# Where an attention pair's high part is made, and when one operand's copy is taken, in a fused attention and two-MoE kernel

## The chip, the cores and the metric

The kernel runs on one core of a Trainium2 chip. The metric is the device time of one execution in microseconds, lower is better. The engines are TensorE (PE in the rows, PEld for its weight loads), VectorE (DVE), ScalarE (ACT), GpSimd (POOL) and SyncE (SP), whose queue issues nearly all transfers.

## What is computed

Attention with a decay, then a mixture of experts with one expert for each token, then a dense two-layer network. Only the attention is touched. Cut from the reference:

```python
def _attn_ref(q, k, v, f):                      # q, k, v: 4 x 8 x 576 x 64
    scores = scale * np.matmul(q, k.transpose(0, 1, 3, 2))
    cum = np.cumsum(np.log(np.clip(f, 0.0001, 1.0)), axis=-1)
    scores = np.where(causal, -1e9, scores + cum[..., :, None] - cum[..., None, :])
    attn = np.exp(scores - np.max(scores, axis=-1, keepdims=True))
    attn = attn / (np.sum(attn, axis=-1, keepdims=True) + 1e-09)
    return np.matmul(attn, v)
x = attn_out.transpose(0, 2, 1, 3).reshape(B * S, H * D)
x = _moe_ref(x, ...)                            # 8 experts, the best one for each token
return _moe2_ref(x, ...)                        # (max(0.01 h, h)) @ w_out, h = x @ w_in
```

## The kernel before

**Pairs of heads.** The 32 heads (4 batches of 8) are worked through as 16 pairs, g = 0 to 15. The 576 rows of a head are five row blocks: 0 to 3 of 128 rows, block 4 of 64 (both heads' block 4 share one tile). A pair's scores come in four groups: blocks 0 and 1 together (`qk01`), then 4, 2 and 3. For each group TensorE forms scores in PSUM (L331, L332, with the mask L334 or L337), VectorE takes the row maxima (`nm`, L341, and L388 for block 4), ScalarE takes exponentials with their row sums (L346, L393). Then TensorE transposes the probabilities (L420, L410), ScalarE copies the transposes to SBUF (L422, L412), and TensorE multiplies them with the values (L432).

**High and low parts.** Scores are made from q and k in two parts. `prep_hi(g)` makes the high part `aq` of a loaded pair on VectorE (L299). It also issues, on SP, three small transfers (L301, L302) and the transfer of half of `aq` to `bk` (L303), and on POOL two copies into the tile for block 4 (L305). `prep_lo(g)` then takes `ak`'s copy of half of `aq` on ScalarE (L312) and the low part on VectorE (L313). On SP it issues L314, L315 and L316, the last of which overwrites the half of `aq` that L312 and L303 read; on POOL one copy (L317).

**Output stage.** `xout(g)` runs a pair later. It sums and inverts the row sums (L448 to L450), TensorE turns the products back (L455), in two halves (row blocks 0 to 2, then 3 and 4), and VectorE scales each half out of PSUM with two instructions, into `x` and into `lp` for the gate (L459).

**Buffers.** The transposes and both halves of the output stage take PSUM tiles in turn from a pool of three (`pst`). So the second transposes of row block 3 use the buffer that the first half of the output stage has to leave. Score tiles take turns in a pool of two (`psc`): the scores of row block 2 use the buffer of blocks 0 and 1, once the exponentials of these have read it.

**Order.** In the attention loop PE, ACT, DVE and SP run in the order in which the code is written; POOL's order is left to the scheduler. For each pair the loop calls `first`, `last`, `third`, `fourth`. `first(g)` makes the scores of blocks 0 and 1 and transposes row block 3 of the pair before (two tiles, four transposes each). `fourth(g)` makes block 3's scores, the transposes of block 2, and the output stage of the pair before; `prep_hi` of the pair two ahead stands in it too. The other halves of the kernel, the experts and the dense network, follow the loop and keep their order.

Of the kernel before, what the change touches and what calls it, by code (L numbers as in the profile page):

```python
# [73 lines left out]
def fused(ctx: ExitStack, tc, qk0, qk2, vp, f, mid, wg, mb, w1, w2, w_in, w_out, out):  # L74
# [71 lines left out]
    with tc.tile_pool(name="pst", bufs=PST, space=PSUM) as pst:  # L146
# [44 lines left out]
        def vload(g):  # L191
            vts[g] = a2.tile([P, 2, NC, D], F32, tag="vt", name=f"vt{g}", bufs=2)
            nc.sync.dma_start(vts[g], vp[:, 2 * g:2 * g + 2])

        def load(g):
            if g == 1:

                xt[0] = pe.tile([P, NC, XW], F32, tag="x", name="x0")
                raw = xt[0].rearrange("p c d -> p (c d)")[:, :2 * S].rearrange("p (h s) -> p h s", h=2)
            else:  # L200
                raw = pe.tile([P, 2, S], F32, tag="raw", name=f"raw{g}", bufs=3)
            nc.sync.dma_start(raw, qk2[:, 2 * g:2 * g + 2, :])
            ops[g] = raw
# [90 lines left out]
        def prep_hi(g):  # L294
            raw = ops[g]
            aq, ak = (aqk.tile([P, 2, S], F32R, tag=n, name=f"{n}{g}") for n in ("aq", "ak"))
            h = aq.bitcast(F32)
            bq, bk, a4, b4 = bqs[g % NBUF], bks[g % NBUF], aq4[g % NBUF], bq4[g % NBUF]
            nc.vector.tensor_scalar(aq, raw, qs, None, ALU.mult)  # L299
            for t, r0, c0 in ((bq, 64, 0), (bk, 66, 2)):  # L300
                nc.sync.dma_start(t[r0:r0 + 2].bitcast(F32), agd[c0:c0 + 2, 2 * g:2 * g + 2, :])  # L301
            nc.sync.dma_start(b4[64:66, :, :64].bitcast(F32), agd[0:2, 2 * g:2 * g + 2, 4 * P:])  # L302
            nc.sync.dma_start(bk[0:64].bitcast(F32), h[64:128])  # L303
            for r in (0, 64):
                nc.gpsimd.tensor_copy(a4[r:r + 64, :, :64], h[0:64, :, 4 * P:])  # L305
            ops[g] = (raw, aq, ak)

        def prep_lo(g):
            raw, aq, ak = ops[g]
            bq, bk, b4 = bqs[g % NBUF], bks[g % NBUF], bq4[g % NBUF]  # L310
            h = aq.bitcast(F32)
            nc.scalar.copy(ak[0:64], h[64:128])  # L312
            nc.vector.scalar_tensor_tensor(raw.bitcast(F32R), raw, qs, h, ALU.mult, ALU.subtract)  # L313
            nc.sync.dma_start(bq[0:64].bitcast(F32), raw[0:64])  # L314
            nc.sync.dma_start(ak[64:128].bitcast(F32), raw[64:128])  # L315
            preps.append(nc.sync.dma_start(h[64:128], h[0:64]))  # L316
            nc.gpsimd.tensor_copy(b4[0:64, :, :64], raw[0:64, :, 4 * P:])  # L317
            ops[g] = (aq, bq, ak, bk)
# [30 lines left out]
        def qk01(g):  # L349
            sc = psc.tile([P, 2, 512], F32, tag="sc", name=f"sc{g}_01")  # L350
            vs = [sc[:, c, :2 * (c + 1) * P].rearrange("p (j k) -> p j k", j=2) for c in range(2)]
            for c, v in enumerate(vs):
                scores(g, c, v)
            nms = [maxima(g, c, v) for c, v in enumerate(vs)]

            def then():
                pt = a3.tile([P, 2, 3 * P], F32, tag="p0", name=f"p{g}_01", bufs=2)
                for c, v in enumerate(vs):
                    exps(g, c, v, nms[c], pt[:, :, c * P:(2 * c + 1) * P])
                    yield  # L360
            return then()

        def qk(g, c):
            n = (c + 1) * P
            view = psc.tile([P, 2, 512], F32, tag="sc", name=f"sc{g}_{c}")[:, :, :n]
            scores(g, c, view)
            nm = maxima(g, c, view)

            def then():
                exps(g, c, view, nm, a3.tile([P, 2, 4 * P], F32, tag="p", name=f"p{g}_{c}", bufs=2)[:, :, :n])  # L370
            return then
# [25 lines left out]
        def part_of(g, part):  # L397
            if (g, part) not in st:
                st[g, part] = a2.tile([P, 2, (3, NC)[part], (XA, XB)[part]], F32, tag=f"t{part}", name=f"tt{g}_{part}", bufs=2 - part)
            return st[g, part]  # L400


        def tr(g, c, js):
            sb = part_of(g, c // 3)
            if c == 4:
                pt = st.pop((g, c, "p"))
                for b0, b1 in ((0, 3), (3, 5)):
                    ps = pst.tile([P, 512], F32, tag="t", name=f"pt{g}_4_{b0}")
                    for b in range(b0, b1):
                        nc.tensor.transpose(ps[:, (b - b0) * P:(b - b0 + 1) * P], pt[:, b * P:(b + 1) * P], ident)  # L410
                    i = ps[:, :(b1 - b0) * P].rearrange("p (b j q) -> p j b q", j=2, q=64)
                    nc.scalar.copy(sb[:, :, b0:b1, P:], i)  # L412
                return
            pt = st[g, c, "p"]
            ps = pst.tile([P, 512], F32, tag="t", name=f"pt{g}_{c}_{js[0]}")
            nb = c + 1
            for i, j in enumerate(js):
                for b in range(nb):
                    k = i * nb + b
                    nc.tensor.transpose(ps[:, k * P:(k + 1) * P], pt[:, j, b * P:(b + 1) * P], ident)  # L420
            o = sb[:, js[0]:js[-1] + 1, 0:nb, c % 3 * P:(c % 3 + 1) * P]
            return lambda: nc.scalar.copy(o, ps[:, :len(js) * nb * P].rearrange("p (j b q) -> p j b q", b=nb, q=P))  # L422
# [14 lines left out]
            st[g, "x", part] = xu  # L437
            nc.vector.tensor_copy(xu[:, :w], pv_[:, :w])

        def xout(g):  # L440
            b, gg = divmod(g, H // 2)
            if gg == 0 and b:
                xt[b] = (pe, pre)[b % 2].tile([P, NC, XW], F32, tag="x", name=f"x{b}")
            x = xt[b]
            lp = lps[b % 2]
            rr = a3.tile([P, NC, 2], F32, tag="rr", name=f"rr{g}")

            nc.vector.tensor_copy(sms[g % 3][:64, 4, 1:2], sms[g % 3][64:, 4, 0:1])  # L448
            nc.vector.tensor_scalar(rr, sms[g % 3], 1e-9, None, ALU.add)
            nc.vector.reciprocal(rr, rr)  # L450
            for part, c0, n in ((0, 0, 3), (1, 3, 2)):
                xu = st.pop((g, "x", part))
                ps = pst.tile([P, 512], F32, tag="t", name=f"xo{g}_{part}")
                for i in range(n):
                    nc.tensor.matmul(ps[:, i * HW:(i + 1) * HW], lhsT=xu[:, i * P:(i + 1) * P], rhs=idw[:, gg, :], start=True, stop=True)  # L455
                i0 = ps[:, :n * HW].rearrange("p (c d) -> p c d", d=HW)
                sc = rr[:, c0:c0 + n, :].unsqueeze(3)
                for o, a, w in ((x[:, c0:c0 + n, gg * P:(gg + 1) * P], slice(0, P), D), (lp[:, c0:c0 + n, gg, :], slice(P, HW), E)):
                    nc.vector.tensor_tensor(o.rearrange("p c (j d) -> p c j d", j=2), i0[:, :, a].rearrange("p c (j d) -> p c j d", j=2), sc.to_broadcast([P, n, 2, w]), ALU.mult)  # L459
            if gg == H // 2 - 1:  # L460
                routing.append(route(b))
                if b == B - 2:
                    routing.append(route1(pre, (B - 1) * NC))
# [80 lines left out]
        def store(n):  # L544
            for _ in range(min(n, len(stores))):
                b, x, c0, c1 = stores.pop(0)
                t0 = b * S + c0 * P
                if c0 == 4:
                    nc.sync.dma_start(xs[t0:(b + 1) * S, :], x[:64, 4, :])
                else:  # L550
                    nc.sync.dma_start(xs[t0:t0 + (c1 - c0) * P, :].rearrange("(c p) d -> p c d", p=P), x[:, c0:c1, :])
# [91 lines left out]
        NG = BH // 2  # L643
# [10 lines left out]
        def first(g):  # L654
            then = qk01(g) if g < NG else None
            cs = [tr(g - 1, 3, (j, )) for j in range(2)] if g else ()
            if g + 1 < NG:
                prep_lo(g + 1)
            store(1 + (g > 12))
            for c in cs:  # L660
                c()
            for _ in then or ():
                pass

# [21 lines left out]
        def fourth(g):  # L686
            then = qk(g, 3) if g < NG else None
            if g + 3 < NG:
                load(g + 3)
            if g + 1 < NG:  # L690
                vload(g + 1)
            if g + 2 < NG:
                prep_hi(g + 2)
            cs = [tr(g, 2, (j, )) for j in range(2)] if then else ()
            for c in cs:
                c()
            if g:
                xout(g - 1)
            if then:
                then()  # L700

# [530 lines left out]
```

## Time and profile before

| | us |
|---|---|
| median of 3 runs | 890.97 |
| lowest, highest | 889.01, 891.54 |
| profiled execution | 889.86 |
| its span, first to last instruction | 888.2 |
| TensorE busy in the span | 853.8 (96%) |
| attention loop from the second pair on | about 24 to 208 of the span |

The rows further down are from one profiled execution. A row of the timeline is: start in us from the span's start, duration in us, engine, line of the kernel, operation, out<-in with the tile names (buffer numbers left out), shape, count of merged instructions, and in brackets the idle time just before on that engine with what ended it. A busy TensorE is not TensorE at its peak, since its instructions overlap.

### The profile page before, as it was taken

Reading aid. Unit: us, or ns where it says so; the run is one execution under the profiler, and the core shown is the slowest. Engines: PE = TensorE matmul, PEld = TensorE weight load, DVE = VectorE, ACT = ScalarE, POOL = GpSimd, SP = SyncE. Lnnn points to the kernel's source line nnn. Section 1 sums busy time; section 2 is a strip of 40 time slices with the busy share of each in tenths; the row PEclk is TensorE's granted clock in tenths of the full one; section 3 lists DMA queues with packets and bytes.
Section 4 is the critical chain, followed back from the end, with each engine's and each line's share of the span. In section 5 each row is a group of like instructions: output and inputs, shape, how many; then the busy total and the mean of one; then the engine's idle time right before and its main releaser. Section 6 shows DMA issues by size and latency. Waiting matters only on the chain. (4 is left out here: it accounts for less than half of the span.)

```text
span 888.2 us, 14348 instructions
## 1 busy us (share of the span) xinstructions
PE 853.8 (96%) x4733; PEld 704.4 (79%) x4733; DVE 601.7 (68%) x1070; ACT 503.7 (57%) x969; POOL 124.9 (14%) x185
## 2 busy tenths in 40 slices
PE   5999999998999999999999999999999999999996
PEld 4788787886788788888787788888888888888885
DVE  6678777886748999999985373386337943473333
ACT  5787778776348899999975353453223422242221
POOL 5000000001112314532231000000000000001112
PEclk9999999999999999999999999999999999999998
DMA  5776786766278145121322240032001300011111
GB/s 153 222 175 183 204 201 180 203 174 221 74 229 285 53 155 166 55 71 51 107 96 64 59 143 13 1 106 84 1 1 48 119 24 0 1 48 48 48 47 72
DMA packets 32994, 92.91 MB, mean 105 GB/s; under 512 B 7349, under 2 KB 8021, under 8 KB 32914
## 3 DMA queue, kind: packets, MB, share of 16 engines
q1 hardware_dynamic: 28082, 76.70, 29.8%
q0 software_dynamic: 4800, 15.23, 5.4%
q8 instruction: 39, 0.64, 0.3%
q14 instruction: 41, 0.34, 0.1%
q10 hardware_dynamic: 32, 0.01, 0.0%
HBM read 132.09 MB, written 14.99 MB: 166 GB/s over the span
## 5 line engine op out<-in xcount | busy, mean ns | idle before, releaser
L1124 ACT COPY us<-u 128x512 f32<-128x512 f32 (+1 forms) x80 | 43.6, 544 | 162.6 <-PE u L1122 162.5
L1125 DVE SCALAR_TENSOR_TENSOR us<-u,us 128x512 f32<-128x512 f32 (+1 forms) x80 | 51.0, 638 | 124.7 <-ACT us L1124 123.1
L1122 PE MATMUL u<-fxl,whii 128*128 128x512 f32 (+1 forms) x320 | 118.0, 369 | 0.0
L1122 PE MATMUL u<-fxh,wloi 128*128 128x512 f32 (+1 forms) x320 | 117.9, 368 | 0.0
L1122 PE MATMUL u<-fxh,whii 128*128 128x512 f32 (+1 forms) x320 | 116.8, 369 | 0.7 <-ACT fxh L764 0.7
L1142 PE MATMUL a<-whio,gh 128*128 128x512 f32 x280 | 109.6, 392 | 0.0
L1142 PE MATMUL a<-wloo,gh 128*128 128x512 f32 x280 | 109.2, 390 | 0.0
L1142 PE MATMUL a<-whio,gl 128*128 128x512 f32 x280 | 103.2, 389 | 0.0
L876 DVE TENSOR_TENSOR w1l<-w1r,w1h 128x1024 fp32r<-128x1024 f32 x72 | 86.3, 1221 | 10.8 <-ACT w1h L875 8.3
L346 ACT ACTIVATE p<-sc,nm 128x128 f32<-128x128 f32 (+3 forms) x128 | 66.2, 527 | 28.9 <-DVE nm L341 27.2
L876 DVE TENSOR_TENSOR w2l<-w2r,w2h 128x1024 fp32r<-128x1024 f32 x68 | 80.2, 1218 | 0.8 <-ACT w2h L875 0.7
L1127 ACT CAST gh<-us 128x512 fp32r<-128x512 f32 (+1 forms) x76 | 44.6, 587 | 58.1 <-DVE us L1125 38.5
L875 ACT CAST w1h<-w1r 128x1024 fp32r<-128x1024 f32 x72 | 73.7, 1055 | 3.6 <-PE h L893 3.6
L1128 DVE TENSOR_TENSOR gl<-us,gh 128x512 fp32r<-128x512 f32 (+1 forms) x76 | 49.3, 648 | 38.5 <-ACT gh L1127 36.4
L875 ACT CAST w2h<-w2r 128x1024 fp32r<-128x1024 f32 x68 | 69.5, 1052 | 4.4 <-PE y L921 2.3
L1122 PEld LDWEIGHTS u<-fxh,whii 128*128 128x128 f32 x320 | 60.2, 188 | 11.0 <-ACT fxh L764 0.9
L1122 PEld LDWEIGHTS u<-fxh,wloi 128*128 128x128 f32 x320 | 60.3, 188 | 10.3
L1122 PEld LDWEIGHTS u<-fxl,whii 128*128 128x128 f32 x320 | 60.3, 188 | 10.3
L341 DVE TENSOR_REDUCE nm<-sc 128x2 f32<-128x256 f32 (+1 forms) x64 | 51.1, 820 | 23.4 <-PE sc L337 21.3
L921 PE MATMUL y<-w2h,hh 128*128 128x512 f32 x160 | 64.8, 405 | 0.0
L1152 POOL DMA_INDIRECT out<-acc,tid x18 | 18.0, 997 | 326.0 <-DVE acc L1149 287.5
L921 PE MATMUL y<-w2h,hl 128*128 128x512 f32 x160 | 63.1, 395 | 0.2 <-DVE hl L914 0.2
(275 smaller groups left out, 1807.6 us busy)
## 6 DMA issues: line engine op xcount, KB each, us to landing
w1r<-w SPq DMA_DIRECT2D x88, 512.0 KB
w2r<-w SPq DMA_DIRECT2D x82, 512.0 KB
rwi<-w_in SPq DMA_DIRECT2D x16, 512.0 KB
rwo<-w_out SPq DMA_DIRECT2D x16, 512.0 KB
raw<-qk SPq DMA_DIRECT2D x14, 576.0 KB
vt<-vp SPq DMA_DIRECT2D x16, 320.0 KB
xr<-yd SPq DMA_DIRECT2D x18, 256.5 KB
bk<-aq SPq DMA_DIRECT2D x15, 288.0 KB
```

What stands on the lines that cost most here:

```text
L341: nc.vector.tensor_reduce(nm, view, axis=AX.X, op=ALU.max, negate=True)
L346: st["exp"] = nc.scalar.activation(pt[:, j, :], view[:, j, :], AF.Exp, bias=nm[:, j:j + 1], scale=1.0, accum_out=sms[g % 3][:, c, j:j + 1])
L875: nc.scalar.copy(hi[k], raw[k])
L876: nc.vector.tensor_tensor(lo[k], raw[k], hi[k].bitcast(F32), ALU.subtract)
L921: nc.tensor.matmul(Yp[t], lhsT=ap[:, k * P:(k + 1) * P], rhs=wp[k // 2][:, k % 2, :], start=(k == 0 and i == 0), stop=(k == NFB - 1 and i ...
L1122: nc.tensor.matmul(ps, lhsT=w[:, c], rhs=x[:, k, :], start=(k == 0 and i == 0), stop=(k == NKB - 1 and i == 2))
L1124: nc.scalar.copy(us, ps)
L1125: nc.vector.scalar_tensor_tensor(us, ps, 0.01, us, ALU.mult, ALU.max)
L1127: nc.scalar.copy(gh, us)
L1128: nc.vector.tensor_sub(gl, us, gh.bitcast(F32))
L1142: nc.tensor.matmul(A[b][i], lhsT=x[:, c], rhs=w, start=(first and m == 0), stop=(last and m == 2))
L1152: d = nc.gpsimd.indirect_dma_start(out=out[:, :], out_offset=bass.IndirectOffsetOnAxis(ap=tid[:, c:c + 1], axis=0), in_=Y[b, i], in_offset ...
```

## The change

Two orders are changed; no instruction is added or removed. `xout` takes a function to call between its halves, and `fourth(g)` hands it `prep_hi(g + 2)`. So the high part, which stood ahead of the transposes of block 2 in the code and thereby ahead of the whole output stage on VectorE, now stands behind the first half's scaling. In `fourth(0)`, which has no output stage, it is called in place. In `first(g)` the copies of the transposes of row block 3 now stand ahead of `prep_lo(g + 1)`, and so ahead of L312.

```diff
-        def xout(g):
+        def xout(g, between=None):
...
+                if part == 0 and between:
+                    between()
...
             cs = [tr(g - 1, 3, (j, )) for j in range(2)] if g else ()
+            for c in cs:
+                c()
             if g + 1 < NG:
                 prep_lo(g + 1)
             store(1 + (g > 12))
-            for c in cs:
-                c()
...
-            if g + 2 < NG:
-                prep_hi(g + 2)
             cs = [tr(g, 2, (j, )) for j in range(2)] if then else ()
             for c in cs:
                 c()
+            hi = (lambda: prep_hi(g + 2)) if g + 2 < NG else None
             if g:
-                xout(g - 1)
+                xout(g - 1, hi)
+            elif hi:
+                hi()
```

The order on TensorE, POOL and SP is the same as before in the whole program. On VectorE 13 instructions move (g = 1 to 13) and on ScalarE 14 (g = 1 to 14).

VectorE in `fourth(1)`, from the maxima of row block 3 to the first maxima of the next pair. `sm` are the row sums, `rr` their inverses, `xo_0` and `xo_1` the two halves in PSUM. Before:

```order
L341 TENSOR_REDUCE nm_3_490<-sc_3_483 128x2
L299 TENSOR_SCALAR aq_496<-raw_350,qs 128x1152
L448 COPY sm_184<-sm_184 64x1
L449 TENSOR_SCALAR rr_515<-sm_184 128x10
L450 RECIPROCAL rr_515<-rr_515 128x10
L459 TENSOR_TENSOR x_209<-xo_0_519,rr_515 128x3x128
L459 TENSOR_TENSOR lp_191<-xo_0_519,rr_515 128x3x16
L459 TENSOR_TENSOR x_209<-xo_1_525,rr_515 128x2x128
L459 TENSOR_TENSOR lp_191<-xo_1_525,rr_515 128x2x16
```

The same place on VectorE after the change:

```order
L341 TENSOR_REDUCE nm_3_490<-sc_3_483 128x2
L448 COPY sm_184<-sm_184 64x1
L449 TENSOR_SCALAR rr_506<-sm_184 128x10
L450 RECIPROCAL rr_506<-rr_506 128x10
L459 TENSOR_TENSOR x_209<-xo_0_510,rr_506 128x3x128
L459 TENSOR_TENSOR lp_191<-xo_0_510,rr_506 128x3x16
L299 TENSOR_SCALAR aq_516<-raw_350,qs 128x1152
L459 TENSOR_TENSOR x_209<-xo_1_525,rr_506 128x2x128
L459 TENSOR_TENSOR lp_191<-xo_1_525,rr_506 128x2x16
```

L299 moved behind the two instructions that empty `xo_0`.

ScalarE around `first(2)`, from the exponentials of row block 3 of pair 1 (`p_3`) to those of blocks 0 and 1 of pair 2 (`p_01`); `pt_3_0` and `pt_3_1` are the two tiles of transposes, `tt_1` where they go. Before:

```order
L346 ACTIVATE p_3_530,sm_185<-sc_3_483,nm_3_490 128x512 x2
L312 CAST ak_497<-aq_496 64x1152
L422 COPY tt_1_548<-pt_3_0_549 128x4x128
L422 COPY tt_1_548<-pt_3_1_554 128x4x128
L346 ACTIVATE p_01_567,sm_186<-sc_01_533,nm_0_544 128x128 x2
```

The same place on ScalarE after the change:

```order
L346 ACTIVATE p_3_530,sm_185<-sc_3_483,nm_3_490 128x512 x2
L422 COPY tt_1_548<-pt_3_0_549 128x4x128
L422 COPY tt_1_548<-pt_3_1_554 128x4x128
L312 CAST ak_517<-aq_516 64x1152
L346 ACTIVATE p_01_567,sm_186<-sc_01_533,nm_0_544 128x128 x2
```

L312 moved behind the two copies, directly ahead of the exponentials.

## Rows read from the trace of the kernel before

**Rows 1.** Waits, 24 to 204 us: engine, line <- releaser: total us, times, longest.

```profile
PE pt L420 <- DVE lp L459: 2.0, 8, 0.4
```

**Rows 2.** Timeline of TensorE, pair 8, transposes of block 3 to the products.

```profile
109.89 0.60 PE L420 MATMUL pt<-ident,p 128*128 128x128 f32 x4
110.70 0.63 PE L420 MATMUL pt<-ident,p 128*128 128x128 f32 x4 [0.22 <-DVE lp L459]
...
114.40 0.44 PE L331 MATMUL sc<-ak,aq 128*128 128x384 f32 x1
...
115.43 1.64 PE L432 MATMUL pv<-tt,vt 128*64 128x192 f32 x20
```

**Rows 3.** Timeline of VectorE, same place: high part, and the first half's last instruction.

```profile
108.27 0.81 DVE L299 TENSOR_SCALAR aq<-raw,qs 128x1152 fp32r<-128x1152 f32 x1
...
110.36 0.20 DVE L459 TENSOR_TENSOR lp<-xo,rr 128x48 f32<-128x48 f32 x1
```

**Rows 4.** Timeline of ScalarE, pair 8, cast to the copies of block 4.

```profile
109.63 0.20 ACT L346 ACTIVATION_READ_ACCUMULATOR p<-sc,nm 128x1 f32 x1
109.86 1.15 ACT L312 CAST ak<-aq 64x1152 fp32r<-64x1152 f32 x1
110.92 1.06 ACT L422 COPY tt<-pt 128x512 f32<-128x512 f32 x2
111.98 0.37 ACT L346 ACTIVATE p<-sc,nm 128x128 f32<-128x128 f32 x1
...
113.49 0.21 ACT L346 ACTIVATION_READ_ACCUMULATOR p<-sc,nm 128x1 f32 x1
113.58 0.76 ACT L412 COPY tt<-pt 128x384 f32<-128x384 f32 x2
```

**Rows 5.** Timeline of TensorE, pair 14: first transposes of block 3, scores of block 2.

```profile
183.91 0.60 PE L420 MATMUL pt<-ident,p 128*128 128x128 f32 x4
...
188.00 0.44 PE L331 MATMUL sc<-ak,aq 128*128 128x384 f32 x1
```

**Rows 6.** Timeline of ScalarE, pair 14: first copy of those transposes.

```profile
184.60 0.59 ACT L422 COPY tt<-pt 128x512 f32<-128x512 f32 x1 [0.35 <-PE pt L420]
```

**Rows 7.** Timeline of ScalarE, pair 7: second copy and first exponential.

```profile
99.56 0.59 ACT L422 COPY tt<-pt 128x512 f32<-128x512 f32 x1
100.17 0.37 ACT L346 ACTIVATE p<-sc,nm 128x128 f32<-128x128 f32 x1
```

**Rows 8.** Timeline of TensorE, pair 9: first transposes of block 3, scores of block 2.

```profile
121.80 0.60 PE L420 MATMUL pt<-ident,p 128*128 128x128 f32 x4
...
126.68 0.44 PE L331 MATMUL sc<-ak,aq 128*128 128x384 f32 x1 [0.30 <-ACT p L346]
```

**Rows 9.** Timeline of ScalarE, pair 9: first and last of the exponentials' rows.

```profile
124.90 0.37 ACT L346 ACTIVATE p<-sc,nm 128x128 f32<-128x128 f32 x1 [1.02 <-DVE nm L341]
...
126.41 0.21 ACT L346 ACTIVATION_READ_ACCUMULATOR p<-sc,nm 128x1 f32 x1
```

**Rows 10.** Timeline of TensorE, pairs 1, 2 and 4, the same two places.

```profile
24.68 1.04 PE L420 MATMUL pt<-ident,p 128*128 128x128 f32 x8
...
29.63 0.44 PE L331 MATMUL sc<-ak,aq 128*128 128x384 f32 x1 [0.33 <-ACT p L346]
...
37.01 0.60 PE L420 MATMUL pt<-ident,p 128*128 128x128 f32 x4
38.03 0.63 PE L420 MATMUL pt<-ident,p 128*128 128x128 f32 x4 [0.42 <-DVE lp L459]
...
41.72 0.44 PE L331 MATMUL sc<-ak,aq 128*128 128x384 f32 x1
...
61.30 1.32 PE L420 MATMUL pt<-ident,p 128*128 128x128 f32 x8
...
65.68 0.44 PE L331 MATMUL sc<-ak,aq 128*128 128x384 f32 x1
```

**Rows 11.** Timeline of SP, pair 8: the last of the low part's transfers.

```profile
114.48 0.73 SPq L316 DMA_DIRECT2D aq<-aq  x1
```

## Prediction

> **What bounds the kernel now.** I read the page first (which engine is busy, and where), then the list of waits for the attention stretch, then the timeline of one pair of heads, engine by engine, and last the same places in the other pairs. TensorE is busy almost without a break in the attention stage, so a gap on it is time lost, and the list of waits shall tell which gap the change aims at: eight times TensorE's transposes (L420) wait for VectorE's last instruction on the first half of the output stage (L459) [rows 1]. In pair 8 the first four transposes of row block 3 start at 109.89 and the next four only at 110.70 [rows 2]; the `lp` instruction that frees their PSUM buffer runs from 110.36 for 0.20 us [rows 3]. Without a wait eight such transposes take 1.04 us (pair 1 [rows 10]); here 110.70 + 0.63 - 109.89 = 1.44, so 0.40 us is lost. I call the start of these transposes T. They are made for the pair before, while pair g starts.
>
> The next thing to see is what the time from T to the scores of row block 2 (L331, "qk2") consists of, because qk2 may start only when ScalarE has read the scores of blocks 0 and 1 out of their buffer (four exponentials, L346). In pair 8: T = 109.89, qk2 = 114.40, 4.51 us [rows 2]; the exponentials end at 113.49 + 0.21 = 113.70 [rows 4], so ScalarE has 0.64 us to spare there (113.70 + 0.06 against 114.40). In pair 9 they end later, and that is where the price of lateness is seen: 126.41 + 0.21 = 126.62 [rows 9], and qk2 starts at 126.68, marked as waiting for ScalarE [rows 8]. So qk2 follows the exponentials' end by 0.06 us, and the slack of pair 8 is all that ScalarE may lose.
>
> **VectorE's part of the change.** In the thirteen output stages with a high part to make, the 0.81 us instruction L299 [rows 3] moves behind the first half. The `lp` that ends at 110.56 then ends about 109.75, before 109.89 + 0.44 = 110.33, when TensorE could start the second four. This wait goes. The work in sum is the same, and I see no new wait on VectorE, so the second half and the maxima behind it end when they did. Users of the high part are later by about 1.6 us: two POOL copies (L305) and SP's transfer L303. All of them are for a pair that starts a whole period later. SP queues three issues behind L303, and the last, L316, stands at 114.48 [rows 11], so a 1.6 us later L303 (near 110.7) holds none of them up. Cost: nothing, the cover being that period.
>
> **ScalarE's part.** Here I differ from what the diff suggests. `ak`'s copy (L312, 1.15 us [rows 4]) no longer runs while TensorE makes the transposes, but after both copies of them. ScalarE now idles from 109.83 until the first four are done, and the cast then stands in front of the exponentials. From T, in rows: the first copy of the transposes starts 0.69 us after T where it waits for TensorE alone (183.91 to 184.60, pair 14 [rows 5, 6]). One copy is 0.59 us and the next starts 0.11 before its end (184.60, and 99.56 for the length of the second [rows 6, 7]), so both are done at 0.69 + 0.59 - 0.11 + 0.59 = 1.76. The cast is 1.15. The exponentials take 113.70 - 111.98 = 1.72 [rows 4]. Then 0.06 to qk2.
>
> The two seams beside the cast are not in the trace in this order. Nearest rows: an instruction behind a copy starts 0.10 us before its end (184.60's kind, and the copy after the cast in pair 8, 109.86 + 1.15 = 111.01 against 110.92 [rows 4]), while the cast itself started 0.03 after its forerunner (109.83 to 109.86 [rows 4]), and the first exponential 0.02 after the copy (99.56 + 0.59 = 100.15 to 100.17 [rows 7]). Together the seams lie between -0.20 and +0.05. Below that there is nothing, since no row shows more overlap. T to qk2 becomes 1.76 + 1.15 + 1.72 + 0.06 = 4.69 with the seams: 4.49 to 4.74. I take 4.60: the seam ahead of the cast as the cast shows it (+0.03), the one behind it as what follows the cast shows it (-0.10), 4.62, rounded a little towards the overlapping rows. TensorE alone could do it in 4.51 - 0.40 = 4.11, so ScalarE decides in every such pair.
>
> **The sum.** T to qk2, before against 4.60:
> - Pairs 6, 8, 10 and 12 have pair 8's form, 4.51 or 4.52: +0.09 or +0.08 each, 0.35 for the four.
> - Pairs 3, 7, 11 and 14 had no wait on `lp` (T came late in them): 4.09 or 4.10, as pair 14, 188.00 - 183.91 [rows 5]. ScalarE had no time to spare for a cast there: +0.50 or +0.51 each, 2.02 for the four.
> - Pairs 5, 9 and 13: 126.68 - 121.80 = 4.88 [rows 8]. The exponentials waited for the maxima on VectorE there, 1.02 us [rows 9], and those do not move: 0.
> - Pair 1: 29.63 - 24.68 = 4.95, since the cast waited for its high part; the copies now fill that time: -0.35. Pair 2: 41.72 - 37.01 = 4.71: -0.11. Pair 4: 65.68 - 61.30 = 4.38: +0.22 [rows 10].
>
> Eleven pairs had 4.95 + 4.71 + 4.38 + 18.05 + 16.38 = 48.47; 11 x 4.60 = 50.60; **+2.1 us**. With 4.49 it is +0.9, with 4.74 +3.7. From qk2 to the next T the order on TensorE and its rows stay, so the loss is passed on. What is late next is the copies L412, which end 0.64 after the exponentials (113.58 + 0.76 = 114.34 [rows 4]); their product starts at 115.43, 1.03 behind qk2 [rows 2], so they stay hidden.
>
> The profiled execution took 889.86 us, 1.1 below the median of 890.97: the sum gives 892.0 on the one and 893.1 on the other. I take a base of 890.4 between them, and **892.5 us**. The bound for a change that can be measured is 0.3%, 2.7 us around 890.97, so the likeliest case counts as no change.
>
> **The rivals.**
> - *TensorE's gap is what counts (faster).* If the exponentials did not hold qk2, the gaps would come back: 0.40 four times, 0.61 in pair 2 (38.03 + 0.63 - 37.01 - 1.04), 0.28 in pair 4 (1.32 - 1.04), 0.35 in pair 1 [rows 2, 10], in sum -2.8, 887.6 us. It needs T to qk2 of 4.11, 0.38 under my lower bound. Eight real waits speak for it, the 0.64 us of slack against a cast of 1.15 against it. The Trainium skill (Perfetto Trace Analysis, Optimization Strategy) reads a gap that repeats on the engine that should be saturated as a sign of too few buffers for the next tile. By that rule freeing the buffer sooner should give this rival's time; the trace agrees that a PSUM buffer is the cause, but shows the next holder close behind.
> - *Both seams drain (slower).* Place: ahead of the cast and behind it on ScalarE. If neither overlaps, T to qk2 is 4.74 and the sum +3.7, 894.1 us. From 4.65 on it is over 2.7 us. For it: the two exact seams of the trace that end in a cast or in these exponentials are +0.03 and +0.02; against it: what follows the cast overlaps by 0.10.
> - *The two cancel (no change).* At 4.41 the sum is nil, 890.4 us. It takes seams shorter than any row.
> - *A transfer comes late.* L316 must follow both the cast and L303. The cast ends at most T + 2.96, 112.85 in pair 8, 1.6 before the issue [rows 11]; L303's landing isn't in these rows. It would show as TensorE waiting for `aq` at a pair's start; above the sum if so.
>
> **How the numbers follow.** ScalarE decides near 4.60, 892.5: 0.58. Both seams drain, 894.1: 0.24. They cancel, 890.4: 0.08. TensorE's gap comes back, 887.6: 0.07. A late transfer, above 894: 0.03. The range takes in the first three with about a microsecond for the spread between runs, 889.8 to 895.0, and leaves out the gap coming back and most of the late transfer. Slower by over 0.3% are the second and the last, 0.27; faster by over 0.3% is the gap coming back, which lies at the very bound, 0.06; the rest, 0.67, is within.
>
> **What will show it.** Right: no wait of L420 for `lp` in pairs 2 to 13; the copies L422 of block 3 waiting some 0.7 us for TensorE in pair 8's kind; L312 directly ahead of the exponentials; qk2 waiting for ScalarE in nearly every pair, about 4.6 us behind T. Wrong: qk2 4.1 to 4.3 behind T (the overlap is larger than I read), TensorE waiting for `aq` transfers, or the maxima on VectorE later than before.

## The result, and the profile after

The changed kernel takes 894.72 us, median of 6 runs (894.27 to 895.68), beside 889.35 (888.69 to 891.54) for the kernel before in runs of the same chip: a ratio of 1.0057, 95% interval 1.0044 to 1.0070. It is slower, by more than the 0.3% named as the bound. The profiled execution took 895.68 with a span of 894.0, against 888.2 before.

TensorE's waits in the attention stretch, 24 to 204 us, answer to [rows 1]. Columns: engine, line <- releaser: total us, times, longest.

```profile
PE sc L331 <- ACT p L346: 8.0, 14, 0.7
PE pt L420 <- ACT tt L422: 0.6, 2, 0.3
PE sc L331 <- DMA aq<-aq: 0.4, 1, 0.4
PE pt L420 <- ACT p L346: 0.2, 1, 0.2
```

The wait of L420 for `lp`, 2.0 us in eight places before, is gone. In its place the scores of row block 2 (qk2) wait for ScalarE's exponentials fourteen times, 8.0 us. Before, that wait stood in the same stretch with 1.7 us, five times:

```profile
PE sc L331 <- ACT p L346: 1.7, 5, 0.5
```

Pair 8 shows one of them, to be laid beside [rows 2]; here is TensorE's timeline.

```profile
112.39 1.04 PE L420 MATMUL pt<-ident,p 128*128 128x128 f32 x8
...
117.13 0.44 PE L331 MATMUL sc<-ak,aq 128*128 128x384 f32 x1 [0.57 <-ACT p L346]
```

The eight transposes now run in one piece of 1.04 us, so the 0.40 us is back. But from their start T to qk2 it is 4.74 us, where it was 4.51. The timeline of VectorE shows how the first part of the change worked: `lp` ends at 112.27, before the transposes start, and the high part stands behind it.

```profile
112.07 0.20 DVE L459 TENSOR_TENSOR lp<-xo,rr 128x48 f32<-128x48 f32 x1
112.18 0.81 DVE L299 TENSOR_SCALAR aq<-raw,qs 128x1152 fp32r<-128x1152 f32 x1
```

ScalarE's timeline at the same place shows where the time goes now (compare [rows 4]). The four exponentials with their row sums start at 115.36; the last row is the end of the last of them.

```profile
113.09 1.07 ACT L422 COPY tt<-pt 128x512 f32<-128x512 f32 x2 [0.75 <-PE pt L420]
114.19 1.15 ACT L312 CAST ak<-aq 64x1152 fp32r<-64x1152 f32 x1
115.36 0.37 ACT L346 ACTIVATE p<-sc,nm 128x128 f32<-128x128 f32 x1
...
116.87 0.21 ACT L346 ACTIVATION_READ_ACCUMULATOR p<-sc,nm 128x1 f32 x1
```

ScalarE stands idle for 0.75 us until the first transposes are done, copies, casts for 1.15 us, and only then takes the exponentials, which end at 117.08. From T: 0.70 + 1.07 + 0.03 (a seam) + 1.15 + 0.02 (a seam) + 1.72 + 0.05 = 4.74. Read at every pair, T to qk2 is 4.74 or 4.75 in ten of the pairs 2 to 14 and 4.81 to 4.83 in pairs 5, 9 and 13.

**Where the 5.8 us of the two spans went.** I mark the stretch by qk2 of pair 1 and qk2 of pair 15. Before it is 29.63 to 200.73, 171.10 us; after 30.77 to 205.08, 174.31. So the loop lost 3.21. The start lost 1.14 (30.77 - 29.63) and the rest, from 205.08 to the span's end, 1.45 (894.0 - 205.08 against 888.2 - 200.73). The loop is the change's, as the experiments show. The two others stand where TensorE runs slower for a while. At the end of the attention its granted clock falls to 0.50 for a while, 1.2 of 2.4 GHz, after a stretch in which it was busy for only 1.6 us in 4 (before) and 1.7 in 4.3 (after). The windows below lie just inside these stretches. Their columns are: stretch, us, then busy time of PE, PEld, DVE, ACT and POOL with counts, granted clock, DMA share, GB/s. In the kernel before the low stretch takes up 3.2 us:

```profile
209.00:213.00 4.00, 1.63 (x12) 1.16 (x11) 3.34 (x5) 4.00 (x5) 0.00 (x0) 1.00 0.81 319
213.20:216.40 3.20, 3.12 (x14) 1.54 (x14) 2.11 (x3) 2.60 (x6) 0.00 (x0) 0.50 0.00 0
```

After the change it takes up 6.8 us:

```profile
214.00:218.30 4.30, 1.68 (x12) 0.94 (x12) 3.95 (x4) 4.30 (x7) 0.00 (x0) 1.00 0.67 263
218.40:225.20 6.80, 6.05 (x36) 4.36 (x33) 2.64 (x7) 2.89 (x6) 0.99 (x1) 0.50 0.14 39
```

At the start it is pair 1's transposes, 1.91 us for eight where [rows 10] have 1.04. The clock's column reads 1.00 around them in this trace, so that a lower clock is not shown here; in the second trace of the change it is (below).

```profile
25.26 1.91 PE L420 MATMUL pt<-ident,p 128*128 128x128 f32 x8
```

The experiments below show that both vary between executions of one kernel.

### The profile page after: what moved, and what is told of

It reads as the page before. It is cut to its first block, busy times and chain, and to the rows that moved or that the text cites. A ratio compares the mean times of both kernels' runs of the same rounds, so it can differ in the third digit from the quotient of the medians.

```text
span 894.0 us, 14348 instructions
## 1 busy us (share of the span) xinstructions
PE 855.7 (96%) x4733; PEld 707.9 (79%) x4733; DVE 600.8 (67%) x1070; ACT 504.9 (56%) x969; POOL 116.6 (13%) x185
## 5 line engine op out<-in xcount | busy, mean ns | idle before, releaser
L924 PE MATMUL y<-w2l,hh 128*128 128x512 f32 x160 | 62.5, 391 | 0.0
```

The source lines that it names most:

```text
L924: nc.tensor.matmul(Yp[t], lhsT=ap[:, k * P:(k + 1) * P], rhs=wp[k // 2][:, k % 2, :], start=(k == 0 and i == 0), stop=(k == NFB - 1 and i ...
```

## The experiments

Theory A: ScalarE's chain of copies, cast and exponentials sets qk2, whatever VectorE does. Its rivals are that VectorE's part, the later high part and what hangs on it, makes the loss, and that the low-clock stretches make it; the letters of the rivals are explained in the expectations where they stand, and are not the same throughout. All medians are set against runs of the kernel before of the same session (891.37 for the first four, 891.69 for the next four, 891.53 for the last two). "Loop" is qk2(1) to qk2(15), 171.10 us before, and stands on one trace of each kernel; the ratio stands on all runs. The ratios are those on record. They are not the quotients of the two medians, and differ from these by up to 0.15%.

| kernel | median us | ratio (95%) | T to qk2, most pairs | loop, change from before |
|---|---|---|---|---|
| VectorE part alone | 890.90 | 0.9995 (0.9983 to 1.0007) | 4.1 to 4.9 | +0.74 |
| ScalarE part alone | 897.85 | 1.0058 (1.0037 to 1.0078) | 5.04 | +5.74 |
| the change again | 895.39 | 1.0047 (1.0032 to 1.0062) | 4.74 | +3.24 |
| early inverse | 885.53 | 0.9930 (0.9916 to 0.9944) | 4.10 | -5.32 |
| half the cast on GpSimd | 891.23 | 1.0001 (0.9982 to 1.0020) | 4.26 | -0.15 |
| cast behind the exponentials | 891.32 | 0.9997 (0.9979 to 1.0015) | 4.10 | +1.57 |
| change and early inverse | 893.77 | 1.0024 (1.0002 to 1.0046) | 4.74 | +2.02 |
| early inverse again | 884.89 | 0.9931 (0.9897 to 0.9964) | 4.10 | -5.66 |
| early inverse, half cast behind | 887.52 | 0.9961 (0.9942 to 0.9980) | 4.26 | -4.13 |
| early inverse, late high part | 887.63 | 0.9957 (0.9937 to 0.9978) | 4.10 | -3.98 |

**VectorE's part alone.** Only `prep_hi` moves between the output stage's halves; the cast stays ahead of the copies.

```diff
-            if g + 2 < NG:
-                prep_hi(g + 2)
...
-                xout(g - 1)
+                xout(g - 1, hi)
```

> The change's VectorE part alone: the high part is made between the halves of the output stage, the cast to ak stays ahead of the copies of block 3's transposes. Theory A (the cast right ahead of the exponentials makes scores of block 2 wait): the cast now waits for the high part, which ends 0.60 us after T, so T to these scores is 0.60 + 0.03 + 1.15 + 1.06 + 1.72 + 0.06, some 4.6 us in pair 8, against 4.51 before and 4.74 after; pairs 3, 7, 11 and 14 stay near 4.1 to 4.2. About +0.6 us to before, 890. The wait of the transposes for lp is gone. Theory B (the later high part is what costs, through VectorE or its transfers): most of the +5.4 us is here, 893 to 895.

No difference: 0.9995. The `lp` wait is gone here too, but the gap that it leaves is taken by other waits: qk2 waits for ScalarE ten times, 3.9 us, since ScalarE's cast waits for VectorE's high part. That wait, 24 to 204 us, and then pair 8: the transposes on TensorE, the high part on VectorE, the cast on ScalarE, and qk2 on TensorE.

```profile
ACT ak L312 <- DVE aq L299: 10.8, 14, 1.4
```

```profile
111.28 1.04 PE L420 MATMUL pt<-ident,p 128*128 128x128 f32 x8
...
110.88 0.81 DVE L299 TENSOR_SCALAR aq<-raw,qs 128x1152 fp32r<-128x1152 f32 x1
...
111.72 1.15 ACT L312 CAST ak<-aq 64x1152 fp32r<-64x1152 f32 x1 [0.69 <-DVE aq L299]
...
115.62 0.44 PE L331 MATMUL sc<-ak,aq 128*128 128x384 f32 x1 [0.17 <-ACT p L346]
```

The cast waits for the very instruction that was moved: it is the same pair's high part, and `first` comes right behind `fourth`. T to qk2 is 115.62 - 111.28 = 4.34 here, where some 4.6 was expected; 4.49 to 4.55 in several other pairs, and up to 5.26 in pair 10. So the two parts of the change belong together: the later high part would hold up a cast that stays where it was.

**ScalarE's part alone.** Only the order in `first` changes.

```diff
+            for c in cs:
+                c()
             if g + 1 < NG:
                 prep_lo(g + 1)
             store(1 + (g > 12))
-            for c in cs:
-                c()
```

> The change's ScalarE part alone: the cast stands behind the copies of block 3's transposes, the high part stays ahead of the output stage. Theory A: the second copy must also wait for the second transposes, which still wait for lp, so T to the scores of block 2 is about 5.0 us in pair 8, 0.3 more than with both parts; in all some +2.4 us to the whole change, about 897. Theory B: no more than 890 to 891.

Slower than the kernel before, and its loop is 2.5 us longer than the whole change's (the ratios of the two overlap). TensorE has both costs in a row: the `lp` wait and then qk2's wait for ScalarE. T to qk2 is 118.96 - 113.92 = 5.04, which is 4.74 and 0.3 of the gap.

```profile
113.92 0.60 PE L420 MATMUL pt<-ident,p 128*128 128x128 f32 x4
114.73 0.63 PE L420 MATMUL pt<-ident,p 128*128 128x128 f32 x4 [0.21 <-DVE lp L459]
...
118.96 0.44 PE L331 MATMUL sc<-ak,aq 128*128 128x384 f32 x1 [0.46 <-ACT p L346]
```

This puts the loss on the cast's place, as A has it.

**The change once more,** without an edit, for a second trace.

> The change itself a second time, for a second trace. T to the scores of block 2 again 4.74 us in nearly every pair and the loop some 3 us longer than before from pair 1 to pair 15 (theory A). The rest of the +5.4 us stood in the first trace at two places where TensorE had its lower clock: pair 1 (full clock from 27.3 us, before from 21.9) and the end of the attention (6.8 us at the low clock, before 3.4). Theory C (these belong to the change): both are there again. Theory D (they fall differently from run to run): at least one is not, and the time stays within 893.5 to 895.5.

The loop is 30.73 to 205.07, +3.24, as in the first trace (+3.21), and T to qk2 is 4.74 again (pair 10 has 4.86). Of the two slow places of the first trace one is there again. At the start the eight transposes of pair 1 take 1.68 us, qk2(1) stands at 30.73 (30.77 in the first trace), and here the granted clock is seen to be 0.50:

```profile
23.40:26.60 3.20, 3.20 (x16) 3.08 (x16) 1.66 (x3) 0.16 (x3) 0.57 (x2) 0.50 1.03 363
```

The stretch at the end of the attention is another one:

```profile
218.00:221.20 3.20, 2.83 (x13) 1.24 (x12) 1.96 (x3) 2.41 (x6) 0.00 (x0) 0.50 0.00 0
```

It takes up 3.2 us, as in the kernel before, and from qk2(15) to the end of the span it takes 687.33 us against 687.47 before. So the 1.45 us of the first trace do not come with every execution of the change. What the start is worth is taken up under the early inverse.

**Early inverse** ("the hoist" in the expectations). The kernel before, with L448 to L450 (the sums of the pair before, long ready) issued ahead of the maxima of row block 3, where VectorE waits for TensorE anyway. L299 and the cast stay.

```diff
         def fourth(g):
+            if g:
+                inverse(g - 1)
             then = qk(g, 3) if g < NG else None
...
-            nc.vector.tensor_copy(sms[g % 3][:64, 4, 1:2], sms[g % 3][64:, 4, 0:1])
-            nc.vector.tensor_scalar(rr, sms[g % 3], 1e-9, None, ALU.add)
-            nc.vector.reciprocal(rr, rr)
+            rr = rrs.pop(g)
```

> Not the change, but another way to its aim: the kernel before, with the three instructions on the row sums (L448 to L450) ahead of block 3's maxima, where VectorE idles 1.57 us in pair 8. High part and cast stay where they were. Theory A: the wait for lp goes (lp ends 0.78 us earlier) and ScalarE's chain stays at T + 3.87, under TensorE's 4.11; pairs 5, 9 and 13 too fall from 4.88 to about 4.1, since the maxima come 0.78 us earlier. In all -3.5 to -5 us, 884 to 886. If the gap on TensorE were worth nothing: 889.

A ratio of 0.9930, faster than both kernels, and in a second session:

> The kernel before with the inverses ahead of the maxima of row block 3, once more on this chip, so that the three others stand beside it: ratio 0.992 to 0.994, 4.1 us from the first transposes of row block 3 to the scores of row block 2. If the gain was that of one run, the ratio is within 0.3% of 1.

0.9931. This is what the change aimed at, reached from the other side. Pair 8 of the second trace, TensorE, then ScalarE, then VectorE:

```profile
109.26 1.04 PE L420 MATMUL pt<-ident,p 128*128 128x128 f32 x8
...
113.36 0.44 PE L331 MATMUL sc<-ak,aq 128*128 128x384 f32 x1
```

```profile
109.24 1.15 ACT L312 CAST ak<-aq 64x1152 fp32r<-64x1152 f32 x1
110.30 1.06 ACT L422 COPY tt<-pt 128x512 f32<-128x512 f32 x2
111.37 0.37 ACT L346 ACTIVATE p<-sc,nm 128x128 f32<-128x128 f32 x1
```

```profile
108.84 0.20 DVE L463 TENSOR_TENSOR lp<-xo,rr 128x48 f32<-128x48 f32 x1
```

`lp` (L463 here) ends at 109.04, ahead of T, so no gap is left; and the cast still fills the time in which ScalarE would wait for the transposes. Qk2 waits for nothing, 4.10 us behind T. That is TensorE's own time: the forecast's 4.11. Pairs 5, 9 and 13 come down from 4.88 to 4.10 too, since the next pair's maxima, which stand behind the output stage on VectorE, no longer have the three instructions ahead of them there.

The two runs of this kernel also settle what the start is worth. Pair 1's transposes took 1.04 us in the one and 1.92 in the other, and qk2(1) stood at 29.62 and 31.62; first the first run's row, then the second's:

```profile
24.69 1.04 PE L420 MATMUL pt<-ident,p 128*128 128x128 f32 x8
```

```profile
25.45 1.92 PE L420 MATMUL pt<-ident,p 128*128 128x128 f32 x8
```

So 2 us of difference at the start come about without any edit, and the change's 1.1 there can't be put down to it.

**Half the cast on GpSimd.** The change, with L312 for head 0 alone on ScalarE and head 1's half on GpSimd.

```diff
-            nc.scalar.copy(ak[0:64], h[64:128])
+            nc.scalar.copy(ak[0:64, 0], h[64:128, 0])
+            nc.gpsimd.tensor_copy(ak[0:64, 1], h[64:128, 1])
```

> The change, with the cast L312 cut in two: ScalarE copies head 0's half of it, GpSimd head 1's half. Theory A (ScalarE's chain copies, cast, exponentials sets the scores of row block 2, L331): the cast of 1152 columns took 1.15 us, a half should take about 0.6, so the time from the first transposes of row block 3 (L420) to those scores goes from 4.74 to about 4.2 in the pairs of the loop, a little above TensorE's own 4.1, with 4.5 to 4.8 left in pairs 5, 9 and 13, which the maxima on VectorE hold. The loop gets about 5 us shorter than the change's: 887 to 889, ratio to the kernel before 0.996 to 0.999. Theory B (the loss comes from another wait, say from the later high part or its transfers): the time from the transposes to the scores may fall, but the loop keeps at least half of its loss, ratio 1.002 or more.

A's first number came out, its time did not, and neither did B's: the ratio of 1.0001 lies between the two. The half takes 0.67 us, and pair 8's qk2 follows T by 116.08 - 111.83 = 4.25. ScalarE, then TensorE (lines from L313 on are one higher here):

```profile
113.62 0.67 ACT L312 CAST ak<-aq 64x576 fp32r<-64x576 f32 x1
```

```profile
111.83 1.04 PE L421 MATMUL pt<-ident,p 128*128 128x128 f32 x8
...
116.08 0.44 PE L332 MATMUL sc<-ak,aq 128*128 128x384 f32 x1
...
123.05 0.30 PE L332 MATMUL sc<-ak,aq 128*128 128x128 f32 x1 [0.53 <-DMA aq<-aq]
...
172.80 0.30 PE L332 MATMUL sc<-ak,aq 128*128 128x128 f32 x1 [1.05 <-DMA aq<-aq]
```

The cast is 0.48 us shorter (1.15 to 0.67), and so is T to qk2 (4.74 to 4.26 in most pairs; pairs 5 and 10, held by VectorE's maxima, have 4.88 and 4.82). Over pairs 2 to 14 the times from T to qk2 add up to 56.68, against 58.17 before, -1.49. But the last two rows give 1.58 back: at the start of pairs 9 and 13 TensorE waits for the transfer that overwrites half of `aq` (L316, L317 here). In the change that wait is 0.4 us, once. Shorter pairs alone are not the reason, as the last two experiments show. The expectation had no such term.

**Cast behind the exponentials.** The change, with `prep_lo` moved once more.

```diff
-            if g + 1 < NG:
-                prep_lo(g + 1)
-            store(1 + (g > 12))
             for _ in then or ():
                 pass
+            if g + 1 < NG:
+                prep_lo(g + 1)
+            store(1 + (g > 12))
```

> The change, with the whole low part (cast L312 among it) behind the exponentials of row blocks 0 and 1 on ScalarE. Theory A: the scores of row block 2 come free, 4.1 us behind the first transposes of row block 3 (4.74 in the change), 4.5 to 4.8 in pairs 5, 9 and 13. The cast of 1.15 us now stands ahead of the copies of block 4's transposes (L412): they end about 1.76 + 1.72 + 1.15 + 0.76 = 5.4 behind the transposes, and the product that needs them stands 1.03 behind the scores, at 5.14, so it waits some 0.3 us in each of 14 pairs, +4 us, against -3.3 for the eleven pairs' scores by the kernel before's 48.47. In sum about +1 against the kernel before, 891 to 893, with TensorE's wait now at the product (L432 for L412) and no longer at L331. Theory B: no difference from the change, 894 to 895.5, with the wait where it was.

As A has it: qk2 comes 4.10 behind T in pair 8 (115.70 - 111.61), and the product that needs the late copies L412 waits instead, though in seven places and not in fourteen. TensorE in pair 8, then its waits, 24 to 204:

```profile
111.61 1.04 PE L420 MATMUL pt<-ident,p 128*128 128x128 f32 x8
...
115.70 0.44 PE L331 MATMUL sc<-ak,aq 128*128 128x384 f32 x1
```

```profile
PE pv L432 <- ACT tt L412: 3.0, 7, 0.5
PE sc L331 <- ACT p L346: 1.9, 4, 0.7
PE sc L331 <- DMA aq<-aq: 0.7, 2, 0.5
```

The loop is +1.57, which would be a ratio of 1.0018; the whole run has 0.9997, with an interval up to 1.0015. The cast has no free place behind the transposes: ahead of the exponentials it holds qk2, behind them the product.

**Change and early inverse together.** The change, with the same edit as in the early inverse.

> The change, with the three instructions that invert the row sums (L448 to L450) ahead of the maxima of row block 3, as in the faster kernel. Theory A: ScalarE's chain decides whatever VectorE does, so the scores of row block 2 stay 4.74 us behind the first transposes of row block 3, now in pairs 5, 9 and 13 too (4.81 to 4.84 before). Against the kernel before the loop has 14 x 4.74 = 66.4 where it had 63.1: +3, ratio 1.003 to 1.005, 893 to 895, nothing of the hoist's 0.7% gain. Theory B (the hoist gains by VectorE's end in itself): most of the gain stays, 889 or less.

The gain of 0.7% is gone: a ratio of 1.0024, whose interval lies above 1 and reaches the expected 1.003 to 1.005, and nowhere near B's 889. TensorE in pair 9, which VectorE's maxima held before at 4.88:

```profile
124.87 1.04 PE L420 MATMUL pt<-ident,p 128*128 128x128 f32 x8
...
129.61 0.44 PE L331 MATMUL sc<-ak,aq 128*128 128x384 f32 x1 [0.57 <-ACT p L346]
```

It is 4.74 here and 4.74 or 4.75 in every pair from 2 to 14. VectorE is earlier than in the change, and ScalarE's chain holds qk2 all the same. This is the plainest of the experiments for A.

**What makes the transfer late.** Two kernels on top of the early inverse: one with the half cast behind the copies and the high part in its old place, one with the late high part and the cast in its old place. Their edits are the ones shown above.

> The kernel before with the inverses L448 to L450 hoisted, the cast L312 behind the copies of the transposes as in the change, and its second half on GpSimd; the high part L299 stays where it was before, ahead of the output stage. In the half-on-GpSimd version of the change the scores of row block 2 came 4.26 us behind the first transposes of row block 3, but TensorE waited for the transfer aq<-aq (L317 there) 0.53 and 1.05 us at the start of pairs 9 and 13, which ate the gain. Theory C (the later high part, and with it the later transfer L303, makes that transfer late): here 4.26 in all pairs from 2 on and none of these waits, the loop 0.16 x 14 = 2.2 us longer than with the hoist alone, 886 to 888, ratio 0.995 to 0.997. Theory D (the later cast, which the transfer must follow, makes it late): the waits of 0.5 us and more stay in two or three pairs, 888 to 889.5.

> The hoist with the VectorE part of the change: L299 between the halves of the output stage, the cast L312 ahead of the copies as before. No lp wait is left for L299 to remove, so only the price of a later high part shows. Theory C: TensorE waits for the transfer aq<-aq 0.5 us and more in two or three pairs, 886 to 888 with 4.1 us from the transposes to the scores, ratio 0.995 to 0.997. Theory D: the late high part is hidden, the waits stay at the 0.2 us of the hoist alone, ratio 0.992 to 0.994, 883.5 to 886.

The first has 4.26 or 4.27 in every pair from 2 to 14 and no wait for `aq`, and its ratio of 0.9961 lies in theory C's range. The loop is 1.2 and 1.5 us longer than in the two traces of the early inverse, where 2.2 was expected. SP's transfers of half of `aq` to `bk` (L303) and within `aq` (L317) start at 108.75 and 113.93 there, 0.77 ahead of and 4.41 behind T = 109.52:

```profile
108.75 0.47 SPq L303 DMA_DIRECT2D bk<-aq  x1
...
113.93 0.46 SPq L317 DMA_DIRECT2D aq<-aq  x1
```

In the half-on-GpSimd version of the change they started 0.62 and 4.60 behind T = 111.83:

```profile
112.45 0.47 SPq L303 DMA_DIRECT2D bk<-aq  x1
...
116.43 0.67 SPq L317 DMA_DIRECT2D aq<-aq  x1
```

The last transfer is issued hardly later; L303 is issued 1.4 us later. When the transfers land is not in these rows. The second kernel gives C half. Its ratio is the one C named, 0.9957, and TensorE waits for `aq` at the start of pair 13, but only there by more than 0.5 us. Another loss stands beside it in pair 10, read from VectorE, ScalarE and TensorE:

```profile
132.64 0.56 DVE L463 TENSOR_TENSOR x<-xo,rr 128x384 f32<-128x384 f32 x1 [1.28 <-DMA xs<-x]
...
133.23 0.81 DVE L299 TENSOR_SCALAR aq<-raw,qs 128x1152 fp32r<-128x1152 f32 x1
```

```profile
134.07 1.15 ACT L312 CAST ak<-aq 64x1152 fp32r<-64x1152 f32 x1 [1.24 <-DVE aq L299]
```

```profile
168.77 0.30 PE L331 MATMUL sc<-ak,aq 128*128 128x128 f32 x1 [0.62 <-DMA aq<-aq]
```

The first scaling of a new batch must wait until the store of an older one has left its buffer; behind the scaling stands the high part, behind this the cast, and T to qk2 is 5.09 there. So a late high part has a price, up to 1 us where it meets something else. The whole change hides most of it under ScalarE's longer chain: its two traces have 4.74 and 4.86 in pair 10. How much of the half-on-GpSimd version's late transfer is the late high part's and how much the early inverse relieves otherwise (it also moves the low part up) these two don't separate.

## Why the prediction came out as it did

**The direction and the mechanism held.** The forecast read that the gap on TensorE would close and bring nothing, because the cast would now stand between the copies and the exponentials that qk2 waits for. Each mark that it named is in the trace: no wait for `lp`, the copies waiting 0.75 us for TensorE (forecast 0.7), L312 directly ahead of the exponentials, qk2 waiting for ScalarE in every pair. The two parts alone, the half cast, the cast behind the exponentials and the change with the early inverse all bear this out.

**The step that failed is the size of the seam behind the cast.** The forecast took 4.60 for T to qk2, with a cast that the exponentials overlap by 0.10. They start 0.02 to 0.03 behind the cast's end, so 0.12 of the missing 0.14 us stands there; the other 0.02 is the forecast's rounding. The seam ahead of the cast was taken rightly from [rows 4], +0.03. Measured is 4.74, the upper bound and the rival "both seams drain". In ten of its eleven pairs (all but pair 1) that rival's sum is 47.40 - 43.52 = +3.88, and the trace has +3.85; with 4.60 it is +2.48.

The nearer row was at hand. The forecast took this seam from what follows the cast in [rows 4], a copy. What follows it in the changed order is an exponential, and [rows 7] have that very exponential behind a copy, at +0.02. But this was no safe choice either: the trace also has another exponential (L393) that overlaps the copy ahead of it by 0.13, more than the forecast's bound, of which it says that "no row shows more overlap". The last section has the rows.

**The time came nearer than the difference.** The forecast stands on a base of 890.4, and the kernel before took 889.35 in the runs beside the changed kernel. So the measured difference is 5.4 us, where +2.1 was put first and +3.7 was the upper bound. That 894.72 lies within the range, near its upper end, owes a microsecond to that base, and this is luck. The loop accounts for 3.2 of the 5.4.

**The sum pair by pair.** The pairs with 4.09 to 4.10 before lost most, +0.64 each where +0.50 was forecast; pair 8's kind +0.23, forecast +0.09; pair 4 +0.36, forecast +0.22. Pairs 5, 9 and 13 fell by 0.05 to 0.06 each, forecast 0. The exponentials still wait for VectorE's maxima there, and these start 0.06 earlier behind T (pair 9: 126.53 - 124.53 = 2.00, before 123.86 - 121.80 = 2.06). Pair 1's gain of 0.35 didn't show: TensorE ran at half its rate there, and the pair took 5.51. From pair 2 on it is 61.86 - 58.17 = +3.69. Of this 0.33 came back at the start of pair 3, where the kernel before had lost it (from qk2(2) to the next T 7.94 us, now 7.61), and small differences make up the rest to the loop's +3.21.

**The chances were wrong in the middle.** The likeliest case stood just inside the bound of 0.3% and the next, 1.6 us above, just outside; a choice of 0.1 us in a seam decided between 0.67 for "no change" and slower.

**Two users of the high part were misjudged.** "All of them are for a pair that starts a whole period later" leaves out the cast, which is a user too and follows in the next call: with VectorE's part alone it waits for L299 fourteen times. In the change nothing of this shows, since the cast was moved away at the same time. The rival of a late transfer had 0.03; the change itself showed no more of it than the kernel before (0.4 us, once), but the half cast on GpSimd lost 1.58 us in this way. It is a real limit close behind.

**What stays open.** The loop's 3.2 us would be a ratio of 1.0036. The second session's interval, 1.0032 to 1.0062, holds it; the first one's, 1.0044 to 1.0070, does not. So a microsecond or two may lie in the stretches ahead of qk2(1) and behind qk2(15), where executions of one kernel differ by as much. Of the twelve traces only those of the kernel before and of the first early inverse have qk2(1) at 29.6; the ten others, both of the change among them, lie between 30.5 and 32.2. With one trace of the kernel before, nothing shows whether the change shifts the odds there.

## What to carry to other kernels

Before closing a gap on the busiest engine, find the next holder of the instruction behind the gap and its slack: here 0.64 us on ScalarE, against a cast of 1.15 that the change put in its way. An engine's idle time ahead of a wait is the place for work that nobody else can cover; the early inverse used VectorE's idle time and left ScalarE's filled, and gained 0.7% where the change lost 0.5%. A seam between two instructions is best priced by a row with the same follower, and even then with a margin: over ten pairs a tenth of a microsecond makes one of the 2.7 us that counted as a change here.

## What the runs showed of the hardware

On ScalarE the time from one instruction's end to the next one's start is not the same everywhere. In the traces before and after, where nothing is waited for, the copies of block 3's transposes start 0.08 to 0.12 us before the end of their forerunner (the cast, or a copy), the cast 0.02 to 0.03 after it, and the first exponential of blocks 0 and 1 0.01 to 0.02 (behind a copy) or 0.02 to 0.03 (behind the cast) after it. This is no rule of the follower alone. L393, the exponential of block 4, starts 0.13 to 0.14 before the end of the copy ahead of it in thirteen pairs of the trace before. In the kernel with the cast behind the exponentials it starts 0.03 after the same copy, while the first exponential of blocks 0 and 1 overlaps its copy by 0.11 in three pairs. Pair 8 before (the copy ends at 114.34, [rows 4]), then pair 9 with the cast behind:

```profile
114.21 0.79 ACT L393 ACTIVATE p<-sc,nm 128x576 f32<-128x576 f32 x1
```

```profile
128.91 0.73 ACT L412 COPY tt<-pt 128x384 f32<-128x384 f32 x2
129.67 0.74 ACT L393 ACTIVATE p<-sc,nm 128x576 f32<-128x576 f32 x1
```

What decides between the two was not tried.

A copy with cast of half the columns (64x576) took 0.67 us, of all (64x1152) 1.15, and GpSimd took as long for the half, 0.67:

```profile
113.25 0.67 POOL L313 CAST ak<-aq 64x576 fp32r<-64x576 f32 x1
```

The stretch at a granted clock of 0.50 at the end of the attention took up 3.2 us in one execution of the changed kernel and 6.8 in another, and the eight transposes of pair 1 took 1.04 us in one and 1.92 in another execution of the same kernel. A difference of 1 or 2 us between two single traces says nothing until its place is known.
